# Threshold attention and hash routing on one core: the scale moves from k to the negation, and the copies of the turned weights get a bias

## The chip, the cores and the metric

One Trainium2 chip, one core. The metric is the device time of one launch in microseconds (us); lower is better. The times of the kernel before are three runs on one chip, and one further execution was recorded by the profiler.

## What is computed

For each of 8 x 8 heads (576 queries, 576 keys, 64 dims) the attention keeps only scores within tau of the row's maximum:

```python
scores = 0.125 * q @ k.T
thresh = scores.max(-1) - tau                       # tau = 0.02
scores = where(scores >= thresh, scores, -1e9)
attn   = exp(scores - scores.max(-1))
attn   = attn / (attn.sum(-1) + 1e-9)
x      = (attn @ v), rows of all heads side by side  # 4608 x 512
```

Then each of the 4608 rows goes to one of 8 experts by a hash of its token id (id times an odd constant, modulo 8), and each expert is `relu(xe @ w1[e]) @ w2[e]` with 512 -> 1024 -> 512. A negative tau would keep no score at all; then every weight of a row is equal (all are -1e9), and the kernel handles that case too.

## The kernel before

The attention runs over 32 pairs of heads (`NP`), and each pair over five query tiles. The engines' order within a pair is written out by hand in the table `ORDER`; an entry is a letter, a tile number and a half, and after the @ how many pairs the operation lags. In the order in which one half-tile passes through them the letters are:

- S (`score`): TensorE multiplies q by k into PSUM, 128 x 576 scores. There are two such PSUM tiles (`sc`).
- N (`negate`): VectorE writes the negated scores `ns` and takes their minimum (`nmx`) in the same operation. GpSimd adds `drop` (tau) to give the threshold `thr`.
- E (`expo`): ScalarE computes `exp(-ns + nmx)`; the minimum comes in as the bias, a tile of one number per partition.
- M (`mask`): VectorE zeroes what is over the threshold and sums the row.
- T (`turn_w`): TensorE turns the masked weights into the PSUM tile `tr`. There is only one such tile, so each T has to wait until the copy before has emptied it.
- P (`put_wT`): ScalarE copies `tr` to SBUF (`wT_a`, `wT_b`). A pair has nine such copies: four of 512 columns a partition, five of 640.
- A and C (`av_part`, `av_tail`): TensorE multiplies the turned weights by v. o (`put_oT`), O (`turn_o`) and X (`put_xm`) copy the result, turn it back, and multiply by the reciprocal of the row sums (R).

K (`scale_k`, line 224) is the operation by which ScalarE multiplies the next pair's k tile, 128 x 704, by `k_scale`: 0.125, or 0 where tau is negative. It stands between P00 and P01. For the first pair, VectorE scales one head's half of k and ScalarE the other (lines 802 and 804) before any score is computed.

The routing of tokens (`route`, lines 390 to 560) is cut into pieces by `yield`; each pair issues one or two pieces between its own operations. A piece holds small operations of VectorE and GpSimd. The one-hot table (288 numbers a partition, line 433) is made by eight compares on GpSimd in three pieces. After the last pair come the entries of `DRAIN`, then the experts' layers.

The places that matter below are named by the letters: T21 is the turn of tile 2's second half, P21 its copy, and so on.

Of the kernel before, what the change touches and what calls it, by code (L numbers as in the profile page):

```python
# [9 lines left out]
FP32 = mybir.dt.float32  # L10
# [3 lines left out]
AF = mybir.ActivationFunctionType  # L14
ALU = mybir.AluOpType
# [5 lines left out]
def kernel(  # L21
# [12 lines left out]
    nc = tc.nc  # L34

    B, H, D, S = qT.shape
    N, DIN = out.shape
    E, _, F = w1.shape
    P = 128
# [4 lines left out]
    NTC = N // P  # L44
    SCALE = 1.0 / float(D) ** 0.5
    assert D == 64 and S == 4 * P + 64 and SCALE == 0.125 and E == 8
    S2 = S // 2
    NQ = 4
    TAIL = NQ * P
    NC = 5  # L50
# [32 lines left out]
    consts = ctx.enter_context(tc.tile_pool(name="consts", bufs=1))  # L83
# [7 lines left out]
    iota_f = consts.tile([P, NOV], FP32, name="iota_f")  # L91
# [2 lines left out]
    slot_i = consts.tile([P, NTC], I32, name="slot_i")  # L94
    tid32 = consts.tile([P, NTC, 2], I32, name="tid32")
    tau_in = consts.tile([P, 1], FP32, name="tau_in")
    k_scale = consts.tile([P, 1], FP32, name="k_scale")
    drop = consts.tile([P, 1], FP32, name="drop")

    stok = consts.tile([P, E, NB], I32, name="stok")  # L100
# [52 lines left out]
    with tc.tile_pool(name="a_q", bufs=1) as a_q, \  # L153
# [27 lines left out]
        summed = [0, 0]  # L181
        kts, rss, recs, scs, nss, stats, ws = {}, {}, {}, {}, {}, {}, {}
# [37 lines left out]
            for j in range(2):  # L220
                nc.sync.dma_start(out=v_sb[64 * j:64 * j + 64, 4], in_=rows[TAIL:S])

        def scale_k(p):
            nc.scalar.activation(kts[p][:], kts[p][:], AF.Copy, scale=k_scale[:])

        def heads(n):
            return 1 if TILES[n % NS] == 0 else 2

# [16 lines left out]
        def negate(n, j):  # L245

            if j == 0:
                nmx = a_st.tile([P, 2], FP32, name="nmx")
                stats[n] = [nmx, None]
            sc = scs.pop((n, j))  # L250
            ns = a_ns.tile([P, S], FP32, name="ns")
            nss[n, j] = ns
            nc.vector.tensor_scalar(out=ns[:].rearrange("p (i s) -> p i s", i=2),  # L253
                                    in0=sc[:, :, 0:S2], scalar1=-1.0, scalar2=None,
                                    op0=ALU.mult, op1=ALU.min,
                                    accum_out=stats[n][0][:, j:j + 1])
            if j == heads(n) - 1:
                thr = a_st.tile([P, 2], FP32, name="thr")
                stats[n][1] = thr
                nc.gpsimd.tensor_scalar(out=thr[:, 0:j + 1], in0=stats[n][0][:, 0:j + 1],  # L260
                                        scalar1=drop[:], scalar2=None, op0=ALU.add)
# [44 lines left out]
        def put_wT(n, j, tr):  # L306
            t = TILES[n % NS]
            if t == 0:
                dst = wT[1][:, :, 0:64].rearrange("p (r c) q -> p r c q", r=2)
                nc.scalar.copy(dst, tr[:, :, 0:64 * NC].rearrange("p r (c q) -> p r c q", c=NC))  # L310
                return
            c0 = P * (t - 1) if t < 3 else 64 + P * (t - 3)
            i0, n_c = ((0, 4), (4, NC))[j]
            dst = wT[t // 3][:, i0:i0 + n_c, c0:c0 + P].rearrange("p c (r q) -> p c r q", r=2)
            nc.scalar.copy(dst, tr[:, :, 0:64 * n_c].rearrange("p r (c q) -> p c r q", c=n_c))  # L315

        def av_part(p, g, chunks):

# [39 lines left out]
        def add_eps(p):  # L358

            rec = a_st.tile([P, 2 * NS], FP32, name="rec")  # L360
            rs = rss.pop(p)
            for i, cols in ((0, 9), (9, 1)):
                nc.gpsimd.tensor_scalar(out=rec[:, i:i + cols], in0=rs[:, i - i // 9:i - i // 9 + cols],
                                        scalar1=1e-9, scalar2=None, op0=ALU.add)
            recs[p] = rec

        def put_xm(p):
# [22 lines left out]
        def route():  # L390
# [3 lines left out]
            keep = rt_sb.tile([P, E, NTC], FP32, name="keep")  # L394
            ones_e = rt_sb.tile([P, E], FP32, name="ones_e")
            eid = rt_sb.tile([P, NTC], I32, name="eid")
            eidf = rt_sb.tile([P, NTC], FP32, name="eidf")
            onehot = rt_sb.tile([P, E, NTC], FP32, name="onehot")
            incl = rt_sb.tile([P, E, NTC], FP32, name="incl")
            row = rt_sb.tile([P, E], BF16, name="row")  # L400
# [25 lines left out]

            nc.vector.tensor_scalar(out=eid[:], in0=tid32[:, :, 0], scalar1=E - 1, scalar2=None,
                                    op0=ALU.bitwise_and)
            nc.gpsimd.tensor_copy(eidf[:], eid[:])
            for e0 in range(0, E, 3):  # L430
                yield
                for e in range(e0, min(e0 + 3, E)):
                    nc.gpsimd.tensor_scalar(out=onehot[:, e], in0=eidf[:], scalar1=float(e),
                                            scalar2=None, op0=ALU.is_equal)
            for e in (0, E // 2):
                yield
                part = slice(e, e + E // 2)
# [4 lines left out]
                if e == 0:  # L442
# [5 lines left out]

            tr = av[:, 0, 320:512]
            nc.tensor.matmul(tr[:, 0:E], lhsT=u128[:], rhs=row[:], start=True, stop=True)
            nc.tensor.matmul(tr[:, E:2 * E], lhsT=ones128[:], rhs=row[:], start=True,
                             stop=True)
            nc.vector.tensor_copy(cnt[:], tr[:, 0:2 * E])
            yield

# [2 lines left out]
                                    scalar2=None, op0=ALU.mult)  # L460
# [3 lines left out]
                                    in1=key[:, :, None].to_broadcast([P, E, E]), op=ALU.is_lt)  # L464
# [3 lines left out]
                                    in1=iota_f[:, 0:E, None].to_broadcast([P, E, E]),  # L468
                                    op=ALU.is_equal)
            nc.gpsimd.tensor_tensor(out=pairs[:], in0=pairs[:],  # L470
                                    in1=iota_f[:, None, 0:E].to_broadcast([P, E, E]),
                                    op=ALU.mult)
            for e0, d in STEPS:
                nc.gpsimd.tensor_scalar(out=more_e[:], in0=pos[:], scalar1=float(e0),
                                        scalar2=float(-d), op0=ALU.is_ge, op1=ALU.mult)
                nc.gpsimd.tensor_tensor(out=cnt[:, E:2 * E], in0=cnt[:, E:2 * E], in1=more_e[:],
                                        op=ALU.add)
            nc.gpsimd.tensor_scalar(out=pos[:], in0=pos[:], scalar1=float(1 << 19), scalar2=-1.0,
                                    op0=ALU.mult, op1=ALU.add)
# [5 lines left out]
                                    scalar2=float(P - 1), op0=ALU.add, op1=ALU.max)  # L485
            nc.vector.tensor_scalar(out=ot_i[:], in0=ot_i[:], scalar1=7, scalar2=None,
                                    op0=ALU.logical_shift_right)
# [4 lines left out]
                                         op1=ALU.add)  # L492
# [5 lines left out]
                                    op0=ALU.mult)  # L498
# [4 lines left out]
                                    in1=base[:, :, None].to_broadcast([P, E, NTC]), op=ALU.add)  # L503
# [207 lines left out]
        def begin(p, s):  # L711
# [21 lines left out]
            if s in (3, 4) or NS * p + s == G0 + NS:  # L733
# [2 lines left out]
        ORDER = """N00@0 S01@0 E41@1 N01@0 O@2 X@2 T21@1 S10@0 S11@0 P21@1 T30@1  # L736
                   A001@1 E00@0 P30@1 E01@0 T40@1 M41@1 N10@0 S20@0 P40@1 N11@0 M00@0
                   S21@0 N20@0 M01@0 T41@1 E10@0 P41@1 A023@1 T00@0 N21@0 M10@0 S30@0
                   E20@0 N30@0 E11@0 C@1 P00@0 T01@0 M11@0 K@-1 S40@0 S41@0 P01@0
                   T10@0 o0@1 N40@0 E30@0 A1012@1 N41@0 P10@0 T11@0 S00@-1 E40@0 R@1  # L740
                   M30@0 M20@0 E21@0 A13@1 M40@0 P11@0 M21@0 T20@0 o1@1 P20@0""".split()
        DRAIN = """E41@1 T21@1 P21@1 O@2 X@2 J J T30@1 P30@1 M41@1 A001@1
                   A023@1 T40@1 P40@1 F F T41@1 P41@1 J F F C@1
                   A1012@1 A13@1 o0@1 o1@1 R@1 F F O@1 X@1""".split()
# [2 lines left out]
        def run_op(p, op):  # L747


            what, lag = op.split("@")  # L750
            kind, args = what[0], [int(c) for c in what[1:] if c.isdigit()]
            q = p - int(lag)
            if kind == "N" and args[1] == 0 and 0 <= p < NP:
                begin(p, args[0])
            if kind == "X" and 0 < p < NP and not placed:
                next(pieces)
            if not 0 <= q < NP:
                return
            n = NS * q + args[0] if kind in "SNEMTP" else 0
            if kind == "S":  # L760
                score(n, args[1])
            elif kind == "N":
                negate(n, args[1])
            elif kind == "E":
                expo(n, args[1])
            elif kind == "M":
                mask(n, args[1])
                if n % NS == NS - 1 and args[1] == 1:
                    add_eps(q)
            elif kind == "T":  # L770
                trs[n, args[1]] = turn_w(n, args[1])
            elif kind == "P":
                put_wT(n, args[1], trs.pop((n, args[1])))
            elif kind == "A":
                av_part(q, args[0], args[1:])
            elif kind == "C":
                av_tail(q)
            elif kind == "o":
                put_oT(args[0])
            elif kind == "O":  # L780
                turn_o()
            elif kind == "X":
                put_xm(q)
            elif kind == "R":
                nc.vector.reciprocal(recs[q][:], recs[q][:])
            elif kind == "K" and q > 0:
                scale_k(q)

        with tc.manual_schedule():
            make_identity(nc, ident[:])  # L790
# [2 lines left out]
            for _ in range(17):  # L793
# [3 lines left out]

            nc.vector.tensor_scalar(out=k_scale[:], in0=tau_in[:], scalar1=0.0, scalar2=SCALE,  # L800
                                    op0=ALU.is_ge, op1=ALU.mult)
            nc.vector.tensor_scalar(out=kts[0][:, 0], in0=kts[0][:, 0], scalar1=k_scale[:],
                                    scalar2=None, op0=ALU.mult)
            nc.scalar.activation(kts[0][:, 1], kts[0][:, 1], AF.Copy, scale=k_scale[:])
            nc.vector.tensor_scalar(out=drop[:], in0=tau_in[:], scalar1=0.0, scalar2=3e38,  # L805
                                    op0=ALU.is_lt, op1=ALU.mult)
            nc.vector.tensor_tensor(out=drop[:], in0=drop[:], in1=tau_in[:], op=ALU.max)
            constants()
            next(pieces)
            for p in range(-1, NP):  # L810
# [630 lines left out]
```

## Time and profile before

| | us |
|---|---|
| median of 3 runs | 911.91 (910.63 to 912.23) |
| profiled execution | 911.19 |
| its span in the trace | 909.6 |
| busy in the span: TensorE / VectorE / ScalarE / GpSimd | 891.1 / 754.1 / 535.1 / 455.0 |

The span is what the trace covers; 1.6 us of the profiled execution lie around it. The attention takes the first half: the last operation of `DRAIN` on TensorE is at 461.5 us. Busy times are sums over the whole span. An operation's busy time runs from its start to its end; two of one engine may overlap by some tens of ns, so the distance of two starts can be shorter than the first one's busy time.

### The profile page before, as it was taken

The page shows a single profiled execution, that of the slowest core. Times are in us where ns is not written, and L with a number is a line of the kernel's source. Part 1 is how long each engine was busy: PE and PEld are TensorE (multiplying, and loading weights), DVE is VectorE, ACT ScalarE, POOL GpSimd, SP SyncE. Part 2 cuts the span into 40 slices and gives each one's busy share as a digit, 9 for nine tenths or more (in the row PEclk, how much of TensorE's full clock was granted, in tenths as well). Part 3 has the DMA queues.
Part 4 walks back from the last instruction along what each step waited for, and adds up shares of the span by engine and source line. Part 5 has one row for each costly group of instructions (what it writes and reads, how often), then busy time and mean ns, then how long its engine had stood idle before and what let it go on. Part 6 is the DMA issues. An engine that isn't in the chain of part 4 may idle for free.

```text
span 909.6 us, 21244 instructions
## 1 busy us (share of the span) xinstructions
PE 891.1 (98%) x7663; PEld 662.6 (73%) x7663; DVE 754.1 (83%) x1697; ACT 535.1 (59%) x879; POOL 455.0 (50%) x672
## 2 busy tenths in 40 slices
PE   7999999999999999999999999999999999999996
PEld 4666665666666666666678989889898988989885
DVE  7999999999999999999855786867777686876831
ACT  5999999999999999999812141423214142141321
POOL 3422333346445423444323496884959679390742
PEclk9999999999999999999999999999999999999999
DMA  7455478975544535642101745373353536421001
GB/s 185 108 148 135 122 208 235 247 213 129 135 113 100 139 78 129 159 123 71 34 26 52 212 137 186 121 219 108 90 181 117 194 119 176 153 74 27 32 23 56
DMA packets 114779, 116.30 MB, mean 128 GB/s; under 512 B 28123, under 2 KB 89315, under 8 KB 114672
## 3 DMA queue, kind: packets, MB, share of 16 engines
q1 hardware_dynamic: 105168, 95.69, 38.7%
q0 software_dynamic: 9072, 18.91, 6.6%
q8 instruction: 62, 1.02, 0.5%
q10 hardware_dynamic: 432, 0.31, 0.1%
q14 instruction: 45, 0.37, 0.1%
HBM read 85.13 MB, written 21.44 MB: 117 GB/s over the span
## 4 chain that ended last, share of the span: by engine, by line
PE 29%; POOL 28%; ACT 19%; issue 17%; DVE 3%; DMA 2%; SPq 1%; POOLq 1%; ACTq 0%; DVEq 0%
POOL out_dram L1264 17%; PE av L323 9%; PE sc L242 8%; ACT w L267 8%; POOL stok_odd L1249 7%; PE tr L289 6%; ACT wT_b L315 6%; POOL xg L120 4%; PE sc L663 3%; ACT wT_a L315 2%; ACT wT_b L310 1%; SPq L1294 1%; DMA q<-in_q_dram 1%; DVE ns L253 1%; ACT oT L346 1%
## 5 line engine op out<-in xcount | busy, mean ns | idle before, releaser
L278 DVE SCALAR_TENSOR_TENSOR w<-ns,thr,w 128x576 f32<-128x576 f32 x288 | 225.8, 808 | 0.0
L267 ACT ACTIVATE w<-ns,nmx 128x576 f32<-128x576 f32 x288 | 217.6, 780 | 3.1 <-DVE ns L253 3.1
L253 DVE TENSOR_SCALAR_CACHE_REDUCE ns<-sc 128x576 f32<-128x576 f32 x288 | 211.1, 752 | 3.4 <-PE sc L242 3.4
L260 POOL TENSOR_SCALAR thr<-nmx,drop 128x2 f32<-128x2 f32 (+1 forms) x160 | 95.4, 596 | 223.1 <-DVE ns L253 192.5
L1264 POOL DMA_INDIRECT out_dram<-o_q,qidx x127 | 148.0, 1166 | 114.0 <-DVE o_q L1255 80.4
L242 PE MATMUL sc<-k_sb,q 64*128 64x288 f32 (+1 forms) x1280 | 187.1, 428 | 2.0 <-DVE drop L805 1.0
L289 PEld LDWEIGHTS tr<-ident,w 64*128 64x128 f32 x2624 | 107.2, 138 | 100.8 <-ACT wT_a L315 43.0
L289 PE MATMUL tr<-ident,w 64*128 64x64 f32 x2624 | 139.9, 231 | 7.2 <-ACT wT_a L315 4.1
L242 PEld LDWEIGHTS sc<-k_sb,q 64*128 64x128 f32 (+1 forms) x1280 | 90.9, 178 | 21.6 <-DVE ns L253 10.7
L315 ACT COPY wT_b<-tr 128x512 f32<-128x512 f32 (+1 forms) x128 | 81.8, 639 | 10.6 <-PE tr L289 5.9
L315 ACT COPY wT_a<-tr 128x512 f32<-128x512 f32 (+1 forms) x128 | 81.2, 634 | 3.5 <-PE tr L289 1.4
L323 PE MATMUL av<-wT_b,v 128*64 128x320 f32 x512 | 82.8, 445 | 0.0
L1249 POOL COPY stok_odd<-stok 128x152 int32<-128x152 int32 x157 | 69.6, 444 | 0.6
L323 PE MATMUL av<-wT_a,v 128*64 128x256 f32 x512 | 69.2, 392 | 0.0
L954 PE MATMUL bank<-h,w_sb 128*128 128x288 f32 (+4 forms) x248 | 62.0, 402 | 0.0
L954 PEld LDWEIGHTS bank<-h,w_sb 128*128 128x128 f32 x248 | 58.7, 291 | 0.5
L954 PE MATMUL sc<-h_s,w_s 128*128 128x288 f32 (+2 forms) x224 | 56.6, 406 | 0.0
L323 PEld LDWEIGHTS av<-wT_b,v 128*64 128x64 f32 x512 | 31.1, 136 | 30.4 <-issue 11.9
L978 ACT ACTIVATE h<-h 128x576 f32<-128x576 f32 (+1 forms) x42 | 29.0, 692 | 41.3 <-DVE h L881 41.2
L120 POOL DMA_INDIRECT xg<-x_scratch,gidx_x x35 | 45.2, 1291 | 12.3 <-DVE xq L1286 5.3
L954 PEld LDWEIGHTS sc<-h_s,w_s 128*128 128x128 f32 x224 | 42.7, 195 | 8.7
L987 ACT COPY p<-sc 128x576 f32<-128x576 f32 (+2 forms) x14 | 9.0, 640 | 55.2 <-PE sc L954 55.2
(241 smaller groups left out, 1462.1 us busy)
## 6 DMA issues: line engine op xcount, KB each, us to landing
w_sb<-in_moe_w_dram SPq DMA_DIRECT2D x16, 2048.0 KB
q<-in_q_dram SPq DMA_DIRECT2D x62, 288.0 KB
v<-in_v_dram SPq DMA_DIRECT2D x32, 256.0 KB
x_scratch<-xm SPq DMA_DIRECT2D x32, 256.0 KB
xT<-xq SPq DMA_DIRECT2D x84, 80.0 KB
k_sb<-in_k_dram SPq DMA_DIRECT2D x31, 176.0 KB
k_sb<-in_k_dram SPq DMA_DIRECT2D x32, 144.0 KB
x_scratch<-xg SPq DMA_DIRECT2D x9, 256.0 KB
```

What stands on the lines that cost most here:

```text
L120: return nc.gpsimd.indirect_dma_start(out=dst, out_offset=None, in_=src, in_offset=bass.IndirectOffsetOnAxis(ap=idx, axis=0), bounds_check ...
L242: nc.tensor.matmul(sc[out_rows, i, 0:S2], lhsT=q_sb[rows, h, q0:q1], rhs=k_sb[rows, h, k0:k0 + S2], start=True, stop=True)
L253: nc.vector.tensor_scalar(out=ns[:].rearrange("p (i s) -> p i s", i=2), in0=sc[:, :, 0:S2], scalar1=-1.0, scalar2=None, op0=ALU.mult, op1= ...
L260: nc.gpsimd.tensor_scalar(out=thr[:, 0:j + 1], in0=stats[n][0][:, 0:j + 1], scalar1=drop[:], scalar2=None, op0=ALU.add)
L267: nc.scalar.activation(w, nss[n, j][:], AF.Exp, bias=stats[n][0][:, j:j + 1], scale=-1.0)
L278: nc.vector.scalar_tensor_tensor(out=w, in0=nss.pop((n, j))[:], scalar=stats[n][1][:, j:j + 1], in1=w, op0=ALU.is_le, op1=ALU.mult, accum_ ...
L289: nc.tensor.transpose(dst[:, r, 64 * c:64 * c + 64], src[rows, c0:c0 + P], ident[rows, rows])
L315: nc.scalar.copy(dst, tr[:, :, 0:64 * n_c].rearrange("p r (c q) -> p c r q", c=n_c))
L323: nc.tensor.matmul(av[64 * j:64 * j + 64, g, 0:width], lhsT=v_sb[:, c, 64 * j:64 * j + 64], rhs=wT[g][:, c + 5 * j, 0:width], start=not su ...
L954: nc.tensor.matmul(ps[:, i], lhsT=lhsT, rhs=y[:, c], start=start and c == 0, stop=c == len(lhsTs) - 1, skip_group_check=not start)
L1249: nc.gpsimd.tensor_copy(stok_odd[:], stok[:])
L1264: inst = nc.gpsimd.indirect_dma_start(out=rows[:, :], out_offset=bass.IndirectOffsetOnAxis(ap=idx, axis=0), in_=o_sb, in_offset=None, boun ...
```

## The change

k is no longer scaled. The factor 0.125 goes into the negation's constant (-1.0 becomes -0.125), so K and the two scalings at the start go away, and the scores' matmuls depend directly on the k transfers. A negative tau is now handled behind the mask: `none_kept` is 1 where tau is negative, else 0, and it is added as a bias tile in the nine P copies, which turn from `copy` (the COPY operation) to `activation` with the Identity function. `drop` gets another form for a negative tau, and the added 1e-9 of the row sums becomes a tile `eps`. The one-hot table becomes one VectorE operation, so the routing has two pieces fewer; one piece more comes from a `yield` between two small matmuls and the copy of their result.

```diff
-        def scale_k(p):
-            nc.scalar.activation(kts[p][:], kts[p][:], AF.Copy, scale=k_scale[:])
...
-                                    in0=sc[:, :, 0:S2], scalar1=-1.0, scalar2=None,
+                                    in0=sc[:, :, 0:S2], scalar1=-SCALE, scalar2=None,
                                     op0=ALU.mult, op1=ALU.min,
...
-                nc.scalar.copy(dst, tr[:, :, 0:64 * NC].rearrange("p r (c q) -> p r c q", c=NC))
+                src = tr[:, :, 0:64 * NC].rearrange("p r (c q) -> p r c q", c=NC)
+                nc.scalar.activation(dst, src, AF.Identity, bias=none_kept[:])
...
-            nc.scalar.copy(dst, tr[:, :, 0:64 * n_c].rearrange("p r (c q) -> p c r q", c=n_c))
+            src = tr[:, :, 0:64 * n_c].rearrange("p r (c q) -> p c r q", c=n_c)
+            nc.scalar.activation(dst, src, AF.Identity, bias=none_kept[:])
...
-                                        scalar1=1e-9, scalar2=None, op0=ALU.add)
+                                        scalar1=eps[:], scalar2=None, op0=ALU.add)
...
-            nc.gpsimd.tensor_copy(eidf[:], eid[:])
-            for e0 in range(0, E, 3):
-                yield
-                for e in range(e0, min(e0 + 3, E)):
-                    nc.gpsimd.tensor_scalar(out=onehot[:, e], in0=eidf[:], scalar1=float(e),
-                                            scalar2=None, op0=ALU.is_equal)
+            yield
+            nc.vector.tensor_tensor(out=onehot[:],
+                                    in0=eid[:, None, :].to_broadcast([P, E, NTC]),
+                                    in1=iota_f[:, 0:E, None].to_broadcast([P, E, NTC]),
+                                    op=ALU.is_equal)
...
+            assert summed[0] in (0, NC)
             tr = av[:, 0, 320:512]
...
+            yield
             nc.vector.tensor_copy(cnt[:], tr[:, 0:2 * E])
...
-                   E20@0 N30@0 E11@0 C@1 P00@0 T01@0 M11@0 K@-1 S40@0 S41@0 P01@0
...
+                   E20@0 N30@0 E11@0 C@1 P00@0 T01@0 M11@0 S40@0 S41@0 P01@0 T10@0
...
-            nc.vector.tensor_scalar(out=k_scale[:], in0=tau_in[:], scalar1=0.0, scalar2=SCALE,
+            nc.vector.tensor_scalar(out=drop[:], in0=tau_in[:], scalar1=0.0, scalar2=-3e38,
+                                    op0=ALU.is_lt, op1=ALU.mult)
+            nc.vector.tensor_tensor(out=drop[:], in0=drop[:], in1=tau_in[:], op=ALU.add)
+            nc.vector.tensor_scalar(out=none_kept[:], in0=tau_in[:], scalar1=0.0, scalar2=-1.0,
                                     op0=ALU.is_ge, op1=ALU.mult)
-            nc.vector.tensor_scalar(out=kts[0][:, 0], in0=kts[0][:, 0], scalar1=k_scale[:],
-                                    scalar2=None, op0=ALU.mult)
-            nc.scalar.activation(kts[0][:, 1], kts[0][:, 1], AF.Copy, scale=k_scale[:])
...
+            nc.vector.tensor_scalar(out=none_kept[:], in0=none_kept[:], scalar1=1.0,
+                                    scalar2=None, op0=ALU.add)
+            nc.vector.tensor_scalar(out=eps[:], in0=none_kept[:], scalar1=float(S), scalar2=1e-9,
+                                    op0=ALU.mult, op1=ALU.add)
```

What this moves on the engines. ScalarE, in a pair in the middle of the attention, from P41 to E30. Before:

```order
L315 COPY wT_b<-tr 128x5x128
L267 ACTIVATE w_132<-ns,nmx 128x576
L267 ACTIVATE w_131<-ns,nmx 128x576
L315 COPY wT_a<-tr 128x4x128
L224 ACTIVATE k_sb<-k_sb,k_scale 128x704
L315 COPY wT_a<-tr 128x5x128
L346 COPY oT<-av 128x256
L267 ACTIVATE w_133<-ns,nmx 128x576
```

And the same place in the changed kernel, where line numbers are up to two lower:

```order
L315 ACTIVATE wT_b<-tr,none_kept 128x5x128
L265 ACTIVATE w_133<-ns,nmx 128x576
L265 ACTIVATE w_132<-ns,nmx 128x576
L315 ACTIVATE wT_a<-tr,none_kept 128x4x128
L315 ACTIVATE wT_a<-tr,none_kept 128x5x128
L346 COPY oT<-av 128x256
L265 ACTIVATE w_134<-ns,nmx 128x576
```

K is gone from between P00 and P01, the copies have an operand more, and nothing else changes its place. The next place is VectorE at the start of the program, from the last memset to the first negations. Before:

```order
L609 MEMSET xg_87 128x512
L800 TENSOR_SCALAR k_scale<-tau_in 128x1
L802 TENSOR_SCALAR k_sb<-k_sb,k_scale 128x352
L805 TENSOR_SCALAR drop<-tau_in 128x1
L807 TENSOR_TENSOR drop<-drop,tau_in 128x1
L253 TENSOR_SCALAR ns,nmx<-sc 128x576 x4
```

And in the changed kernel:

```order
L609 MEMSET xg_88 128x512
L798 TENSOR_SCALAR drop<-tau_in 128x1
L800 TENSOR_TENSOR drop<-drop,tau_in 128x1
L801 TENSOR_SCALAR none_kept<-tau_in 128x1
L803 TENSOR_SCALAR none_kept<-none_kept 128x1
L805 TENSOR_SCALAR eps<-none_kept 128x1
L251 TENSOR_SCALAR ns,nmx<-sc 128x576 x4
```

The scaling of k has gone, and five operations of one number per partition stand where four operations stood. The last place is VectorE in the third pair of the changed kernel, where the one-hot table is now made:

```order
L251 TENSOR_SCALAR ns,nmx<-sc 128x576 x2
L429 TENSOR_TENSOR onehot<-eid,iota_f 128x288
L372 TENSOR_TENSOR xm<-av,rec 128x640
L276 SCALAR_TENSOR_TENSOR w_132,rs<-ns,thr,w_132 128x576
L251 TENSOR_SCALAR ns,nmx<-sc 128x576 x2
```

In the kernel before, L372 follows the negations at that place directly, and the table was made by L433 on GpSimd.

## Rows read from the trace of the kernel before

**Rows 1.** Busy time in one steady pair: window, length, PE, PEld, DVE, ACT, POOL; clock, DMA.

```profile
298.17:311.86 13.69, 13.63 (x176) 8.59 (x174) 13.69 (x39) 12.97 (x23) 7.03 (x11) 1.00 0.40 104
```

**Rows 2.** Waits of VectorE up to 470 us: total, times, longest.

```profile
DVE ns L253 <- PE sc L242: 3.4, 11, 0.8
```

**Rows 3.** The chain of waits through the same pair: start, us, what.

```profile
298.17 0.58 ACT wT_b L315
...
299.44 0.68 ACT wT_b L315
...
300.80 0.68 ACT wT_b L310
...
303.53 0.69 ACT wT_b L315
...
305.46 0.58 ACT wT_a L315
...
306.09 0.53 PE tr L289 x10
```

**Rows 4.** TensorE in that pair, in order of time: T21, T30, T40, T10.

```profile
298.81 0.53 PE L289 MATMUL tr<-ident,w 64*128 64x64 f32 x10
...
300.19 0.50 PE L289 MATMUL tr<-ident,w 64*128 64x64 f32 x10
...
301.64 0.46 PE L289 MATMUL tr<-ident,w 64*128 64x64 f32 x8
...
307.48 0.44 PE L289 MATMUL tr<-ident,w 64*128 64x64 f32 x8
```

**Rows 5.** ScalarE around K: P00, K and P01 of the last pair but one.

```profile
429.56 0.57 ACT L315 COPY wT_a<-tr 128x512 f32<-128x512 f32 x1
430.02 0.89 ACT L224 ACTIVATE k_sb<-k_sb,k_scale 128x704 f32<-128x704 f32 x1
430.81 0.69 ACT L315 COPY wT_a<-tr 128x640 f32<-128x640 f32 x1
```

**Rows 6.** ScalarE's groups over the span, shapes apart: busy us, mean ns, idle before.

```profile
L267 ACT ACTIVATE w<-ns,nmx 128x576 f32<-128x576 f32 x288 | 217.6, 780 | 3.1 <-DVE ns L253 3.1
...
L315 ACT COPY wT_a<-tr 128x640 f32<-128x640 f32 x64 | 44.1, 690 | 3.5 <-PE tr L289 1.4
...
L978 ACT ACTIVATE h<-h 128x576 f32<-128x576 f32 x24 | 16.3, 684 | 23.5 <-DVE h L881 23.5
...
L987 ACT COPY p<-sc 128x576 f32<-128x576 f32 x8 | 5.1, 638 | 29.8 <-PE sc L954 29.8
...
L1011 ACT ACTIVATE h<-bank 128x576 f32<-128x576 f32 x4 | 2.6, 653 | 1.9 <-PE bank L954 1.9
```

**Rows 7.** ScalarE in the last pair, which has no K: P00 and P01.

```profile
443.25 0.58 ACT L315 COPY wT_a<-tr 128x512 f32<-128x512 f32 x1
444.50 0.69 ACT L315 COPY wT_a<-tr 128x640 f32<-128x640 f32 x1 [0.68 <-PE tr L289]
```

**Rows 8.** ScalarE in order of time: P20 of the first, fifteenth and last pair.

```profile
18.68 0.58 ACT L315 COPY wT_b<-tr 128x512 f32<-128x512 f32 x1 [0.70 <-PE tr L289]
...
215.73 0.59 ACT L315 COPY wT_b<-tr 128x512 f32<-128x512 f32 x1
...
449.33 0.58 ACT L315 COPY wT_b<-tr 128x512 f32<-128x512 f32 x1 [0.18 <-PE tr L289]
```

**Rows 9.** The start in order of time: k's scaling, first scores, first negation.

```profile
5.11 0.15 DVE L800 TENSOR_SCALAR k_scale<-tau_in 128x1 f32<-128x1 f32 x1 [3.41 <-DMA tau_in<-in_tau_dram]
...
5.72 0.40 DVE L802 TENSOR_SCALAR k_sb<-k_sb,k_scale 128x352 f32<-128x352 f32 x1 [0.46 <-DMA k_sb<-in_k_dram]
...
6.18 1.31 PE L242 MATMUL sc<-k_sb,q 64*128 64x288 f32 x8 [1.03 <-DVE drop L805]
...
7.04 0.76 DVE L253 TENSOR_SCALAR_CACHE_REDUCE ns<-sc 128x576 f32<-128x576 f32 x1 [0.66 <-PE sc L242]
```

**Rows 10.** VectorE's groups up to 480 us: the compare of route that is nearest in size.

```profile
L549 DVE TENSOR_TENSOR keep<-iota_f,oend 128x256 f32<-128x256 f32 x1 | 0.4, 427 | 0.0
```

More of the change, by code (lines that the diff above doesn't have):

```diff
@@ L96 @@
     tau_in = consts.tile([P, 1], FP32, name="tau_in")
-    k_scale = consts.tile([P, 1], FP32, name="k_scale")
+    none_kept = consts.tile([P, 1], FP32, name="none_kept")
+    eps = consts.tile([P, 1], FP32, name="eps")
     drop = consts.tile([P, 1], FP32, name="drop")
@@ L396, in route @@
             eid = rt_sb.tile([P, NTC], I32, name="eid")
-            eidf = rt_sb.tile([P, NTC], FP32, name="eidf")
             onehot = rt_sb.tile([P, E, NTC], FP32, name="onehot")
@@ L738 @@
                    S21@0 N20@0 M01@0 T41@1 E10@0 P41@1 A023@1 T00@0 N21@0 M10@0 S30@0
-                   E20@0 N30@0 E11@0 C@1 P00@0 T01@0 M11@0 K@-1 S40@0 S41@0 P01@0
-                   T10@0 o0@1 N40@0 E30@0 A1012@1 N41@0 P10@0 T11@0 S00@-1 E40@0 R@1
-                   M30@0 M20@0 E21@0 A13@1 M40@0 P11@0 M21@0 T20@0 o1@1 P20@0""".split()
+                   E20@0 N30@0 E11@0 C@1 P00@0 T01@0 M11@0 S40@0 S41@0 P01@0 T10@0
+                   o0@1 N40@0 E30@0 A1012@1 N41@0 P10@0 T11@0 S00@-1 E40@0 R@1 M30@0
+                   M20@0 E21@0 A13@1 M40@0 P11@0 M21@0 T20@0 o1@1 P20@0""".split()
         DRAIN = """E41@1 T21@1 P21@1 O@2 X@2 J J T30@1 P30@1 M41@1 A001@1
@@ L785, in run_op @@
                 nc.vector.reciprocal(recs[q][:], recs[q][:])
-            elif kind == "K" and q > 0:
-                scale_k(q)
         with tc.manual_schedule():
@@ L796 @@
                                 in_=bass.AP(tensor=tau.tensor, offset=0, ap=[[0, P], [1, 1]]))
-            nc.vector.tensor_scalar(out=k_scale[:], in0=tau_in[:], scalar1=0.0, scalar2=SCALE,
+            nc.vector.tensor_scalar(out=drop[:], in0=tau_in[:], scalar1=0.0, scalar2=-3e38,
+                                    op0=ALU.is_lt, op1=ALU.mult)
+            nc.vector.tensor_tensor(out=drop[:], in0=drop[:], in1=tau_in[:], op=ALU.add)
+            nc.vector.tensor_scalar(out=none_kept[:], in0=tau_in[:], scalar1=0.0, scalar2=-1.0,
                                     op0=ALU.is_ge, op1=ALU.mult)
-            nc.vector.tensor_scalar(out=kts[0][:, 0], in0=kts[0][:, 0], scalar1=k_scale[:],
-                                    scalar2=None, op0=ALU.mult)
-            nc.scalar.activation(kts[0][:, 1], kts[0][:, 1], AF.Copy, scale=k_scale[:])
-            nc.vector.tensor_scalar(out=drop[:], in0=tau_in[:], scalar1=0.0, scalar2=3e38,
-                                    op0=ALU.is_lt, op1=ALU.mult)
-            nc.vector.tensor_tensor(out=drop[:], in0=drop[:], in1=tau_in[:], op=ALU.max)
+            nc.vector.tensor_scalar(out=none_kept[:], in0=none_kept[:], scalar1=1.0,
+                                    scalar2=None, op0=ALU.add)
+            nc.vector.tensor_scalar(out=eps[:], in0=none_kept[:], scalar1=float(S), scalar2=1e-9,
+                                    op0=ALU.mult, op1=ALU.add)
             constants()
```

## Prediction

> **What bounds the kernel now.** I first read the busy times of one steady pair [rows 1]: of 13.69 us VectorE is busy 13.69, TensorE 13.63 and ScalarE 12.97. Three engines look full, so shares alone decide nothing. Second, the waits: VectorE, the fullest, waited for scores only 3.4 us in all of the attention [rows 2]. Less work on VectorE could give that back and no more, unless its own operations get fewer. Third, the chain of waits through that pair [rows 3], and here the reader is to see that it runs through ScalarE and TensorE: P20, E41, P21, E00, P30 and so on, to P00, T01, and from there through TensorE's scores and products to the next P20. Six of the nine P copies stand in it: P20, P21, P30, P40, P41, P00. The reason is the single `tr` tile: a turn can't start before the copy of the turn before has ended, and TensorE, which runs in order, holds the next scores behind that turn. So the loop of copies and turns and VectorE's own work take the same 13.69 us, and whatever makes the loop longer shows up in full, while what makes it shorter meets VectorE.
>
> How tight each tie is, by end of the copy and start of the turn behind it [rows 3, 4]. P00 ends at 306.04 and T01 starts at 306.09, so 0.05 us is what the hand-over takes. P20 ends at 298.75, T21 starts at 298.81: slack 0.01. P21 ends at 300.12, T30 starts at 300.19: 0.02. P30 ends at 301.48, T40 starts at 301.64: 0.11. P01 starts 1.25 after P00 [rows 5], so here at 306.71; it lasts 0.69 and ends at 307.40, and T10 starts at 307.48: 0.03. From P41's start at 303.53 to P00's at 305.46 are 1.93 us, which is P41 and two exps back to back (0.69 + 2 x 0.78 [rows 6], less three overlaps of 0.11): no slack either.
>
> **K goes.** 31 operations of 0.89 us leave ScalarE. I take their worth as nothing, and the last pair says so, since it has no K: there too P01 starts 1.25 us after P00 (443.25 to 444.50) and waits for TensorE's turn [rows 7]; with K it starts 1.25 after P00 as well (429.56 to 430.81) [rows 5]. K lies in a hole that T01 makes. If the hole were smaller than it looks, the gain would end at VectorE: the waits of 3.4 us.
>
> **The copies get a bias tile.** This is the term that decides. No row shows an Identity with a bias tile from PSUM, so I bound it. ScalarE's exp with a bias tile takes 780 ns, its relu without one 684, both over 576 numbers from SBUF to SBUF: 96 ns for the bias tile. Relu from PSUM takes 653, a COPY of the same size from PSUM 638: 15 ns for the other operation [rows 6]. Together 0.11 us a copy, 690 becoming about 800. The lower bound is 0.015, if the bias is read while the copy waits for its turn anyway; the upper is 780 - 638 = 0.14, exp against COPY. I take 0.11, since the two differences are of the same operand and the same memory as here.
>
> The Trainium skill bears on this, in "ScalarE: Activation LUTs", section "What ACT_TABLE_LOAD costs": it says that each operand given as one number per partition adds about 93 ns to an ACTIVATE, against constants in the instruction. The trace's 96 ns agree. By that figure the copy would grow by 0.093 + 0.015, and the sum below would come out 0.3 us lower.
>
> On ScalarE's total: nine copies grow by 0.11 each, 1.0 us a pair, and K gives back 0.8, its distance to P01; 12.97 + 0.2 still lies under 13.69. So ScalarE does not become full; what grows is the loop. P20, P21, P41, P00 and P01 pass on 0.11 each less their slack of 0.06 together: 0.49. P30's slack takes its 0.11, and P40 I treat alike. P10 and P11 have products of 1 us and more between them and the next turn. So **0.49 us a pair**. This stands in front of T01, so the scores of tile 4 come late, and VectorE, which has no work of its own to spare there, waits in N40 by that much.
>
> From the first P20 to the last are 31 intervals, 430.65 us [rows 8]; 31 x 13.69 are 424.4. Of the 6.3 more, the first fourteen intervals hold 5.4 (197.05 - 191.66), the later seventeen 0.9. The early part is the routing's small operations on VectorE (and the start). When VectorE waits half a us a pair, they fall into that wait. I take 3.0 us of it as hidden from now on; bounds 0 and 5.4. That gives 31 x 0.49 - 3.0 = +12.2.
>
> **The drain.** Four copies stand between the last P20 and the end of the turns, partly with other work between: +0.4 (4 x 0.11), bounds 0 and 0.6.
>
> **The start.** The first scores waited for VectorE to scale k, from 5.72, when k was there, to 6.18 [rows 9]. Without that they can start at 5.72: -0.45. The five operations on tau take some 0.15 each from 5.11 on, and end by 5.9, before the first negation (7.04 - 0.46 = 6.58). Bounds: 0, if the q transfers landed only then, and -0.9, if only those two of the three k transfers that the first scores read are early.
>
> **The rest.** The one-hot operation on VectorE: 427 ns for 256 numbers [rows 10] makes 0.48 for 288, at the place of a negation's end in the third pair. It falls into VectorE's new wait, so 0; if that cover is gone, +0.4 (less the overlap). GpSimd loses eight compares and nobody waited for them. The 1e-9 as a tile on GpSimd is followed by the reciprocal far later: 0. The routing ends a piece earlier, which moves transfers that nobody waits for. The negation's constant costs nothing.
>
> **Sum.** +12.2 + 0.4 - 0.45 = +12.15 on the profiled execution's 911.19 (span 909.6 and 1.6 around it): 923.3. That execution lies 0.7 under the median of the runs, within their range; on the median, 911.9, the sum makes **924.0**, which I predict.
>
> **Rivals.**
> 1. The bias tile costs only the lower bound, 0.015. The slack of 0.06 takes nearly all of 5 x 0.015; the one-hot then shows with +0.4, the start gives -0.45: 912.4 (911.9 + 0.5 + 0.4 - 0.45), no change. For it: the copies wait for turns, and an operand could be fetched meanwhile. Against it: the exps wait for minima too, and show the full 780.
> 2. Half of the ties give way, since times jitter between pairs and VectorE still sets the pace of some: 31 x 0.25 less 2 us of hidden routing, +0.2 - 0.45: +5.5, 917.4. For it: VectorE is as full as the loop [rows 1], so the ties may be its making. Against it: the chain of waits never passes through VectorE there.
> 3. Faster: K's 0.8 us a pair frees the loop at P01, with the bias tile nearly free. Then VectorE's waits of 3.4 us go and 0.45 at the start: 908.1. It decides only if P01 starts less than 1.25 us after P00; the last pair without K speaks against it.
> 4. The bias tile costs 0.14: 5 x 0.14 - 0.06 + 2 x 0.03 (what P30 and P40 then pass on) = 0.70 a pair, 21.7 - 3.4 + 0.6 - 0.45 = +18.5: 930.4.
>
> **How the numbers follow.** Forecast 0.68; rival 2 0.15; rival 4 0.06; rival 1 0.07; rival 3 0.04. The forecast's own range, with 0.45 to 0.55 a pair and 1 to 4.5 us hidden, is 921 to 927. The range reaches to rival 2 on the lower side and stops between forecast and rival 4 on the upper: 915.5 to 928; rivals 1, 3 and 4 stay outside. A change under 0.2% (1.8 us) can't be told from none here. Faster: rival 3 and a part of rival 1, 0.05; same: 0.07; slower: 0.88.
>
> **What would show it.** The P copies at about 0.80 us (640) and 0.69 (512); a steady pair of about 14.2 us where it was 13.69; VectorE idle by about 0.5 us a pair before N40, put down to the scores; P01 no earlier after P00 than T01 lets it; the first negation near 6.6 us; the experts' half unchanged in length. If the copies stay at 0.70, the forecast is wrong at its main term; if they grow and the pair stays under 14.0, the ties were looser than I read them. A lower clock on TensorE, from its longer waits, would make it slower than all of this.

## The result, and the profile after

| | before | changed |
|---|---|---|
| median, us (four runs each) | 911.46 (910.63 to 912.23) | 924.86 (923.71 to 925.72) |
| profiled execution, span | 911.19, 909.6 | 925.15, 923.6 |
| ratio | | 1.0141, 95% interval 1.0126 to 1.0156 |

The change makes the kernel 1.4% slower, as predicted (924.0, range 915.5 to 928). Its profile is read here in the order of the prediction's views.

The busy time of a steady pair of the changed kernel, in the columns of [rows 1]:

```profile
305.90:320.17 14.27, 14.02 (x176) 8.53 (x174) 13.82 (x39) 13.11 (x22) 7.19 (x11) 1.00 0.42 104
```

The pair has grown from 13.69 to 14.27 us, on the same clock. VectorE, which had no idle time in [rows 1], now has 0.45, and ScalarE is still not full: 13.11 of 14.27. An engine total would not have shown this slowdown coming. ScalarE's operations over the whole span, in the columns of [rows 6]:

```profile
L265 ACT ACTIVATE w<-ns,nmx 128x576 f32<-128x576 f32 x288 | 215.0, 770 | 4.5 <-DVE ns L251 4.5
L315 ACT ACTIVATE wT_b<-tr,none_kept 128x640 f32<-128x640 f32 x64 | 50.8, 794 | 3.0 <-PE tr L287 1.3 <-ACT w L265 0.3
...
L315 ACT ACTIVATE wT_b<-tr,none_kept 128x512 f32<-128x512 f32 x64 | 44.0, 688 | 1.7 <-PE tr L287 1.6
```

A P copy of 640 numbers a partition takes 794 ns where it took 690: +104, predicted +110. The chain of waits through the same pair shows where that lands:

```profile
305.90 0.69 ACT wT_b L315
...
307.27 0.79 ACT wT_b L315
...
308.75 0.79 ACT wT_b L309
...
311.53 0.79 ACT wT_b L315
312.32 1.33 ACT w L265 x2
313.65 0.59 ACT wT_a L315
...
314.28 0.53 PE tr L287 x10
...
320.17 0.69 ACT wT_b L315
```

It is the chain of [rows 3] again: P20, P21, P30, P40, P41, two exps, P00, T01, and by TensorE to the next P20. What is longer in it, by 0.1 us each, are the copies. TensorE's turns in that pair, T21, T30, T40, T01 and T10:

```profile
306.65 0.53 PE L287 MATMUL tr<-ident,w 64*128 64x64 f32 x10
...
308.12 0.52 PE L287 MATMUL tr<-ident,w 64*128 64x64 f32 x10
...
309.59 0.46 PE L287 MATMUL tr<-ident,w 64*128 64x64 f32 x8
...
314.28 0.53 PE L287 MATMUL tr<-ident,w 64*128 64x64 f32 x10 [0.25 <-ACT wT_a L315]
...
315.75 0.46 PE L287 MATMUL tr<-ident,w 64*128 64x64 f32 x8
```

Counted from the start of P20 and set against [rows 3, 4], the delay builds up one tie after another. T21 starts 0.75 after it (before 0.64), T30 2.22 (2.02), T40 3.69 (3.47), T01 8.38 (7.92), T10 9.85 (9.31), and the next P20 14.27 (13.69). So P20 adds 0.11, P21 0.09, P30 0.02, the stretch with P40, P41 and P00 0.24, P01 0.08, and what follows 0.04. Within that stretch P41 starts 5.63 after P20 (before 5.36) and P00 7.65 (7.29; its row 313.55 stands below), so P40 and the exp between it and P41 bring 0.05, P41 0.09 and P00 0.10. On ScalarE, the place where K stood:

```profile
313.55 0.67 ACT L315 ACTIVATE wT_a<-tr,none_kept 128x512 f32<-128x512 f32 x1
314.90 0.79 ACT L315 ACTIVATE wT_a<-tr,none_kept 128x640 f32<-128x640 f32 x1 [0.68 <-PE tr L287]
```

K's hole of [rows 5] is now 0.68 us of idle time, ended by T01. P01 follows P00 by 1.35 us, later than the 1.25 with K, because P00 itself is longer. VectorE's waits up to 470 us, and the one in this pair, before N40:

```profile
DVE ns L251 <- PE sc L240: 10.5, 31, 0.8
```
```profile
315.39 0.76 DVE L251 TENSOR_SCALAR_CACHE_REDUCE ns<-sc 128x576 f32<-128x576 f32 x1 [0.34 <-PE sc L240]
```

VectorE waited for scores 11 times in [rows 2] and 31 times now, once a pair: 10.5 us where it was 3.4. The wait before N40 is 0.34 of the 0.45 us that VectorE is idle in this pair; most of the rest is a gap of 0.11 before N01. Last, P20 of the first, second, fifteenth and last pair, and the start with the one-hot operation:

```profile
18.54 0.69 ACT L315 ACTIVATE wT_b<-tr,none_kept 128x512 f32<-128x512 f32 x1 [0.56 <-PE tr L287]
...
33.87 0.69 ACT L315 ACTIVATE wT_b<-tr,none_kept 128x512 f32<-128x512 f32 x1
...
220.03 0.69 ACT L315 ACTIVATE wT_b<-tr,none_kept 128x512 f32<-128x512 f32 x1
...
463.07 0.69 ACT L315 ACTIVATE wT_b<-tr,none_kept 128x512 f32<-128x512 f32 x1 [0.29 <-PE tr L287]
```
```profile
5.70 1.48 PE L240 MATMUL sc<-k_sb,q 64*128 64x288 f32 x8 [0.45 <-DMA q<-in_q_dram]
...
6.74 0.76 DVE L251 TENSOR_SCALAR_CACHE_REDUCE ns<-sc 128x576 f32<-128x576 f32 x1 [0.76 <-PE sc L240]
```
```profile
L429 DVE TENSOR_TENSOR onehot<-eid,iota_f x1: 452/452/452, 35.0 to 35.0; 128x288 f32<-128x288 int32 x1
```

From the first P20 to the last are 444.53 us, 13.9 more than the 430.65 of [rows 8]; that is the whole slowdown but for some tenths.

### The profile page after: what moved, and what is told of

The parts are those of the page before. It is cut to its first block, busy times and chain, and to the rows that moved or that the text cites. A ratio compares the mean times of both kernels' runs of the same rounds, so it can differ in the third digit from the quotient of the medians.

```text
span 923.6 us, 21173 instructions
## 1 busy us (share of the span) xinstructions
PE 900.8 (98%) x7663; PEld 661.5 (72%) x7663; DVE 757.8 (82%) x1699; ACT 538.9 (58%) x847; POOL 459.3 (50%) x663
## 4 chain that ended last, share of the span: by engine, by line
POOL 27%; PE 27%; ACT 26%; issue 15%; DVE 2%; SPq 1%; DMA 1%; POOLq 1%; ACTq 0%; DVEq 0%
POOL out_dram L1263 16%; ACT w L265 12%; PE av L323 9%; ACT wT_b L315 9%; POOL stok_odd L1248 7%; PE sc L240 7%; PE tr L287 6%; POOL xg L121 4%; PE sc L663 2%; ACT wT_a L315 2%; ACT wT_b L309 2%; SPq L1293 1%; ACT oT L346 1%; DVE ns L251 0%; POOLq L1263 0%
## 5 line engine op out<-in xcount | busy, mean ns | idle before, releaser
L251 DVE TENSOR_SCALAR_CACHE_REDUCE ns<-sc 128x576 f32<-128x576 f32 x288 | 212.0, 753 | 13.6 <-PE sc L240 10.5
L265 ACT ACTIVATE w<-ns,nmx 128x576 f32<-128x576 f32 x288 | 215.0, 770 | 4.5 <-DVE ns L251 4.5
L258 POOL TENSOR_SCALAR thr<-nmx,drop 128x2 f32<-128x2 f32 (+1 forms) x160 | 99.1, 619 | 236.0 <-DVE ns L251 193.5
L287 PEld LDWEIGHTS tr<-ident,w 64*128 64x128 f32 x2624 | 104.8, 138 | 119.7 <-ACT wT_a L315 52.5
L240 PE MATMUL sc<-k_sb,q 64*128 64x288 f32 (+1 forms) x1280 | 184.8, 425 | 1.3 <-DVE ns L251 0.8
L287 PE MATMUL tr<-ident,w 64*128 64x64 f32 x2624 | 142.9, 233 | 12.1 <-ACT wT_a L315 10.5
L315 ACT ACTIVATE wT_a<-tr,none_kept 128x512 f32<-128x512 f32 (+1 forms) x128 | 94.3, 737 | 22.2 <-PE tr L287 21.9
L240 PEld LDWEIGHTS sc<-k_sb,q 64*128 64x128 f32 (+1 forms) x1280 | 93.0, 178 | 16.4 <-DVE ns L251 4.4
L315 ACT ACTIVATE wT_b<-tr,none_kept 128x512 f32<-128x512 f32 (+1 forms) x128 | 94.8, 741 | 4.6 <-PE tr L287 2.9
```

Of the source, the lines that this page charges most:

```text
L240: nc.tensor.matmul(sc[out_rows, i, 0:S2], lhsT=q_sb[rows, h, q0:q1], rhs=k_sb[rows, h, k0:k0 + S2], start=True, stop=True)
L265: nc.scalar.activation(w, nss[n, j][:], AF.Exp, bias=stats[n][0][:, j:j + 1], scale=-1.0)
L287: nc.tensor.transpose(dst[:, r, 64 * c:64 * c + 64], src[rows, c0:c0 + P], ident[rows, rows])
L315: nc.scalar.activation(dst, src, AF.Identity, bias=none_kept[:])
```

## Experiments

Pair lengths below are the distances of two steady P20 or P00 starts. Every ratio is against the kernel before in the same series of runs.

**1. The copies without the bias.** The changed kernel with the copies as before. Here and in runs 2, 5 and 7 only one of the two places at which a copy is issued is shown; the other changes alike.

```diff
-            nc.scalar.activation(dst, src, AF.Identity, bias=none_kept[:])
+            nc.scalar.copy(dst, src)
```

> The changed kernel with the nine P copies as COPY again, without the bias; everything else of the change stays (it leaves out only the handling of a negative tau). Theory (the bias lengthens the loop of copies and turns): the copies fall back to 0.69 and 0.58 us, a steady pair from 14.27 to 13.69 to 13.72 us, the start keeps its 0.3 us, the one-hot on VectorE shows with up to 0.4: 911.6 us, within 1 us of the kernel before. Rival (another part of the change made it slow: the scores waiting directly on the k transfers, the other constant in the negation, or the routing's moved pieces): a pair stays at 14.2 and the time above 920 us.

Measured: 910.3 us (909.12 to 911.34, 12 runs) against 911.77; ratio 0.9986, 0.9977 to 0.9994. The pair is 13.70 us. ScalarE's P00, P01 and the next P00:

```profile
429.18 0.57 ACT L315 COPY wT_a<-tr 128x512 f32<-128x512 f32 x1
430.43 0.69 ACT L315 COPY wT_a<-tr 128x640 f32<-128x640 f32 x1 [0.68 <-PE tr L287]
...
442.88 0.57 ACT L315 COPY wT_a<-tr 128x512 f32<-128x512 f32 x1
```

Everything else of the change together, K's 0.89 us a pair included, is worth 1.5 us in all by the medians (0.5 to 2.1 by the interval), a little more than the 1 us that was expected at most, and nothing in a steady pair. P01 starts 1.25 after P00, as with K. The whole slowdown is in the nine copies.

**2. The operation without the operand.** Identity with a constant in place of the tile.

```diff
-            nc.scalar.activation(dst, src, AF.Identity, bias=none_kept[:])
+            nc.scalar.activation(dst, src, AF.Identity)
```

> The changed kernel with the copies as Identity, but with the bias as a constant of the instruction (0) and not as a tile (it leaves out the handling of a negative tau). Theory (the operand costs 0.096 of the 0.105 us, the operation 0.01 to 0.015): copies of 0.70 and 0.60 us, whose 5 x 0.015 the slack of 0.06 nearly takes; a pair of 13.69 to 13.75 us and 911.6 to 913 us. Rival (the other operation is what costs, whatever its bias): copies of 0.79, a pair of 14.27 and 924.9 us.

Measured: 910.8 us, ratio 0.9998 (0.9989 to 1.0007), pair 13.77. Its copies:

```profile
L315 ACT ACTIVATE wT_b<-tr 128x640 f32<-128x640 f32 x64 | 45.0, 703 | 6.4 <-PE tr L287 3.9 <-ACT w L265 0.3
...
L315 ACT ACTIVATE wT_b<-tr 128x512 f32<-128x512 f32 x64 | 38.3, 598 | 2.9 <-PE tr L287 1.6
```

With a constant a copy of 640 takes 703 ns, with COPY in run 1 693, with the tile 794. So the tile costs 91 ns and the other operation 10. The prediction's two differences, 96 and 15, were both a little large. The pair came out just above the expected 13.69 to 13.75 us and the time below the expected 911.6 to 913. "ScalarE: Activation LUTs" of the Trainium skill, section "What ACT_TABLE_LOAD costs", states about 93 ns for such an operand; the trace agrees, with 91 here from PSUM.

**3 and 4. Which of the nine.** The bias on P30, P40, P10 and P11 alone, or on P20, P21, P41, P00 and P01 alone, the others as `copy`. Run 3's form, of which run 4 has the other list, `((2, 0), (2, 1), (4, 1), (0, 0), (0, 1))`:

```diff
+        def put_copy(n, j, dst, src):
+            if (n % NS, j) in ((3, 0), (4, 0), (1, 0), (1, 1)):
+                nc.scalar.activation(dst, src, AF.Identity, bias=none_kept[:])
+            else:
+                nc.scalar.copy(dst, src)
```

> The changed kernel with the bias on only the four copies whose slack before the next turn is read as 0.1 us or more (P30, P40, P10, P11), the other five as COPY. Theory (only the tied copies count): 0 to 0.04 us a pair, 911.6 to 913 us. Rival (every copy's 0.1 us costs alike, through ScalarE's total): 4/9 of the 13.4 us lost, 917.5 us.

> The changed kernel with the bias on only the five copies read as tied (P20, P21, P41, P00, P01), the other four as COPY. Theory: nearly all of the loss stays: a pair of 14.22 to 14.27 us, 923 to 925 us. Rival (every copy's 0.1 us costs alike): 5/9 of 13.4, 919 us.

Measured: the four slack copies 911.0 us (ratio 0.9992, 0.9983 to 1.0001; pair 13.75), the five tied ones 923.29 us (ratio 1.0130, 1.0115 to 1.0144; pair 14.22). ScalarE with the five, from P20 to the next P20:

```profile
305.19 0.69 ACT L306 ACTIVATE wT_b<-tr,none_kept 128x512 f32<-128x512 f32 x1
...
308.02 0.69 ACT L308 COPY wT_b<-tr 128x640 f32<-128x640 f32 x1
...
312.79 0.67 ACT L306 ACTIVATE wT_a<-tr,none_kept 128x512 f32<-128x512 f32 x1
...
314.15 0.79 ACT L306 ACTIVATE wT_a<-tr,none_kept 128x640 f32<-128x640 f32 x1 [0.68 <-PE tr L287]
...
319.41 0.69 ACT L306 ACTIVATE wT_b<-tr,none_kept 128x512 f32<-128x512 f32 x1
```

Against run 1's 13.70 the five tied copies add 0.52 a pair and the four slack ones 0.05; together 0.57, as the full change does. The slack copies' 0.05 lies just above the expected 0 to 0.04. The same operand at the same price costs 13.0 us in one set of places and 0.7 in the other (923.29 and 911.0 less 910.3). The reading of ties by the end of a copy and the start of the turn behind it is what the two runs test, and it holds. The rival of both expectations, that every copy's 0.1 us costs alike (917.5 and 919 us), falls.

**5. The bias alone, with K left in.** The kernel before, with a tile of zeros as the bias of the nine copies.

```diff
-            nc.scalar.copy(dst, tr[:, :, 0:64 * n_c].rearrange("p r (c q) -> p c r q", c=n_c))
+            src = tr[:, :, 0:64 * n_c].rearrange("p r (c q) -> p c r q", c=n_c)
+            nc.scalar.activation(dst, src, AF.Identity, bias=zero_b[:])
```

> The kernel before with one edit: the nine P copies as Identity with a bias tile of zeros; K stays. Theory (K lies in the hole that T01 makes, also when P00 is longer: P01 starts 1.35 us after P00 in the changed kernel, and P00's 0.58 and K's 0.79 to the next start make 1.37): a pair of 14.27 to 14.30, P01 1.35 to 1.37 after P00, 924 to 926.5 us. Rival (leaving K out paid for a part of the bias, 0.2 us a pair or more): a pair of 14.47 or more and 931 us or more.

Measured: 926.17 us (925.7 to 927.21), ratio 1.0159 (1.0142 to 1.0176), pair 14.28. P00, K and P01, and the P20 on either side:

```profile
307.49 0.69 ACT L318 ACTIVATE wT_b<-tr,zero_b 128x512 f32<-128x512 f32 x1
...
315.15 0.67 ACT L318 ACTIVATE wT_a<-tr,zero_b 128x512 f32<-128x512 f32 x1
315.71 0.88 ACT L225 ACTIVATE k_sb<-k_sb,k_scale 128x704 f32<-128x704 f32 x1
316.50 0.79 ACT L318 ACTIVATE wT_a<-tr,zero_b 128x640 f32<-128x640 f32 x1
...
321.77 0.69 ACT L318 ACTIVATE wT_b<-tr,zero_b 128x512 f32<-128x512 f32 x1
```

With K between them, P01 starts 1.35 after P00, exactly as in the changed kernel, which has no K. In run 1 VectorE's own work fills the pair, which could have hidden a gain from K; here the loop is longer than that work, and the pair is still that of the changed kernel. So K is worth nothing in a steady pair on either side.

**6. The factor elsewhere.** The kernel before without K: the factor, -0.125 or 0, goes as a tile into VectorE's negation, where a negative tau is then handled too. The copies stay.

```diff
-                                    in0=sc[:, :, 0:S2], scalar1=-1.0, scalar2=None,
+                                    in0=sc[:, :, 0:S2], scalar1=k_scale[:], scalar2=None,
...
-                   E20@0 N30@0 E11@0 C@1 P00@0 T01@0 M11@0 K@-1 S40@0 S41@0 P01@0
+                   E20@0 N30@0 E11@0 C@1 P00@0 T01@0 M11@0 S40@0 S41@0 P01@0
...
```

> The kernel before without K and without the scalings at the start: the factor (-0.125, or 0 for a negative tau) is read by the negation as a tile of one number per partition; copies, routing and everything else as before, all of the reference computed. Theory (such an operand is free on VectorE, where the mask has one already; K is worth nothing; the start gives 0.3): negation of 0.75 us, a pair of 13.69, 910 to 911.5 us. Rival (the operand costs on VectorE as on ScalarE, 0.096 us): negation of 0.85, VectorE's own work 13.6 + 0.86 = 14.5 a pair, some 935 us.

Measured: 922.31 us (922.0 to 923.11), ratio 1.0121 (1.0104 to 1.0137). Both expectations missed. The negation's group on VectorE in the kernel before, then here with its accumulator's reading, and the busy time of a pair:

```profile
L253 DVE TENSOR_SCALAR_CACHE_REDUCE ns<-sc 128x576 f32<-128x576 f32 x288 | 211.1, 752 | 3.4 <-PE sc L242 3.4
```
```profile
L253 DVE TENSOR_SCALAR_CACHE_REDUCE ns<-sc,k_scale 128x576 f32<-128x576 f32 x288 | 225.5, 805 | 1.6 <-PE sc L242 1.4
...
L253 DVE DVE_READ_ACCUMULATOR ns<-sc,k_scale 128x1 f32 x288 | 21.8, 76 | 0.0
```
```profile
299.40:313.50 14.10, 14.05 (x178) 8.53 (x174) 14.10 (x39) 12.29 (x21) 7.11 (x12) 1.00 0.45 113
```

A tile costs VectorE something as well: 805 ns where the constant took 752, +53, neither nothing nor ScalarE's 96. Nine of them, with the accumulator's reading 6 ns shorter (82 to 76), make 9 x 0.047 = 0.42 a pair; the pair grew by 0.41, from 13.69 to 14.10, and VectorE is busy for all of it. The fault in the expectation was to treat the operand as free on the engine that had no slack. With waits of 3.4 us in all [rows 1, 2], VectorE has next to nothing to give, and what it gets shows in full.

**7. The operand twice.** The changed kernel with a tile of ones as the copies' scale as well.

```diff
-            nc.scalar.activation(dst, src, AF.Identity, bias=none_kept[:])
+            nc.scalar.activation(dst, src, AF.Identity, bias=none_kept[:], scale=one_s[:])
```

> The changed kernel with a second operand tile in the nine P copies: a scale of ones beside the bias. Theory (each operand tile lengthens a copy by 0.093, and the loop by that times the tied copies): copies of 0.89 and 0.78 us; five tied copies, and P30 and P40, whose slack is used up, make seven: a pair of 14.73 (five) to 14.92 us (seven), 939 to 945 us. Rival (a second operand is read along with the first): copies of 0.79, a pair of 14.27, 924.9 us.

Measured: 950.67 us (949.98 to 951.76) against 917.21 for the kernel before in that series, which was on a chip where that kernel too took longer; ratio 1.0362 (1.0334 to 1.0389). The expected 939 to 945 us are missed as they stand; 1.0362 of the 911.46 us of the kernel before would be 944.5. The copies, the P20 at either end of an early pair, and a later stretch:

```profile
L316 ACT ACTIVATE wT_b<-tr,none_kept,one_s 128x640 f32<-128x640 f32 x64 | 56.6, 884 | 6.3 <-PE tr L288 5.0 <-issue 0.3
```
```profile
168.45 0.78 ACT L316 ACTIVATE wT_b<-tr,none_kept,one_s 128x512 f32<-128x512 f32 x1
...
183.34 0.78 ACT L316 ACTIVATE wT_b<-tr,none_kept,one_s 128x512 f32<-128x512 f32 x1
```
```profile
255.21:270.82 15.61, 14.37 (x176) 8.54 (x178) 13.91 (x39) 13.82 (x21) 7.64 (x11) 1.00 0.42 103
```

The second tile costs 90 ns, like the first. From 34 to 213 us eleven of the twelve pairs take 14.9 us, like the one shown with 14.89. That is 0.62 more, as if nearly seven copies passed their growth on (0.62 / 0.09). That fits what was expected: once the first operand has used up the slack, the copies that had some are tied too. No run puts the second operand on some of the copies alone, so which seven isn't shown. Not expected was what follows. From 228 to 368 us the pairs take 15.1 to 15.8 us with the same operations on TensorE and VectorE and at the granted clock of 1.00, and of the eight behind them only two are back at 14.9. In the long pairs the chain of waits runs through TensorE's turns and products rather than through the exps behind P20 and P21. What sets it off isn't settled. On this chip the kernel before took 5.5 us longer too, and no trace of it there was kept, so the long pairs may belong to the chip as well as to the edit.

**8. K on another engine.** The kernel before, with K on GpSimd.

```diff
-            nc.scalar.activation(kts[p][:], kts[p][:], AF.Copy, scale=k_scale[:])
+            nc.gpsimd.tensor_scalar(out=kts[p][:], in0=kts[p][:], scalar1=k_scale[:],
+                                    scalar2=None, op0=ALU.mult)
```

> The kernel before with K on GpSimd in place of ScalarE, at the same place of the order; everything of the reference is computed. Theory (K cost nothing on ScalarE): a pair of 13.69 us and 911 to 912 us, provided that GpSimd's multiplication of 704 numbers (some 2 us, from 0.79 us for 288 in the routing) doesn't hold up the thresholds behind it; if it does, VectorE waits for thr by up to 1 us a pair and the time goes up to 940. Rival (ScalarE's 0.8 us a pair was worth something): a pair under 13.6 and less than 909 us.

Measured: 932.76 us (932.18 to 936.34) against 917.21; ratio 1.0163 (1.0140 to 1.0186). It is the expectation's second case, in which K holds up the thresholds. K on GpSimd, its queue in one pair, and what VectorE now waits for up to 480 us:

```profile
L224 POOL TENSOR_SCALAR k_sb<-k_sb,k_scale 128x704 f32<-128x704 f32 x31 | 63.8, 2057 | 0.0
```
```profile
308.49 2.06 POOL L224 TENSOR_SCALAR k_sb<-k_sb,k_scale 128x704 f32<-128x704 f32 x1
310.72 1.03 POOL L568 DMA_INDIRECT slot_scratch<-tok,slot_i  x1 [0.17 <-issue]
311.80 0.31 POOL L261 TENSOR_SCALAR thr<-nmx,drop 128x2 f32<-128x2 f32 x1
```
```profile
DVE w L279 <- POOL thr L261: 12.9, 22, 1.3
DVE ns L254 <- PE sc L243: 9.6, 21, 2.0
```

K takes 2.06 us there, and a threshold that M needs stands in GpSimd's queue behind it: 22 waits of VectorE, 12.9 us. Five more waits before M, 3.9 us, are put down to no releaser. But it isn't K alone. In 15 of the 31 pairs an operation of the routing that issues a transfer, 1.0 to 1.6 us long, stands between K and the threshold, as in the pair shown; 14.4 of these 16.8 us of waiting fall there. Where the threshold follows K directly, M waits 0.19 us at most. GpSimd is busy for only 55% of the span (515.3 of 934.7 us) and still can't take K at this place, since what counts is what else is queued there. Where K costs nothing is the hole on ScalarE in which it stood. No version here handles a negative tau and is faster than the kernel before; run 1, which is 0.14% faster, leaves that out.

## Why the prediction was right

- **The bias tile's price** was predicted at 0.11 a copy; it is 0.104 (794 less 690), 0.091 of it the tile and about 0.01 the other operation (run 2). The lower bound, a tile read while the copy waits anyway (rival 1), falls: the copies in the chain show the full price.
- **0.49 us a pair** was too small; it is 0.575 (two pairs of 14.27 and 14.26, less 13.69). The five ties were sized right: in the pair above they bring 0.11, 0.09, 0.09, 0.10 and 0.08, 0.47 in all against 0.49. Their slack was smaller than the 0.06 that I took off, since after P20, P21 and P01 (ends 306.59, 308.06, 315.69) the turns still start 0.06 later (306.65, 308.12, 315.75), but the copies grew by a little less than 0.11 too. What was mis-sized is what I put at nothing. P30 brings 0.02 and P40 with the exp behind it 0.05. I treated P40 like P30, whose slack is before the next turn, but P41 follows P40 on ScalarE with one exp between them. Run 3, with the tile on P30, P40, P10 and P11 alone, has 0.05 a pair. The last 0.04 arise between T10 and the next P20, and their cause isn't settled: it takes 4.42 us from T10 to there, before 4.38, and also 4.42 in run 4, where P10 and P11 have no bias. Run 4's 0.52 is about the five ties and this. VectorE's wait stands before N40, where it was put, but with 0.34 us and not 0.49.
- **Routing hidden, 3.0 us**, with bounds of 0 and 5.4. Of the 444.53 us, 31 pairs of 14.265 are 442.2, which leaves 2.3 where [rows 8] left 6.3: 4.0 are gone, 3.6 of them in the first fourteen intervals. How much of it the wait hides isn't settled. In runs 1, 2 and 3, with the changed routing and hardly any wait, the same sum leaves 4.1, 4.1 and 4.7 (428.81 less 31 x 13.70; 430.98 less 31 x 13.77; 430.94 less 31 x 13.75), so about half may lie in the other pieces of routing (run 1's first P20 came 1.6 us later than here). In run 5, with the routing of before and the wait, it leaves 2.1 (444.76 less 31 x 14.28), but its first P20 came 1.8 us later than here, which may hold a part.
- These two errors run against each other: 31 x 0.575 - 4.0 = 13.8 between the first and the last P20, predicted 12.2. That the median fell within 0.9 us of 924.0 is in part luck: the slowdown is 13.4 us where the sum had 12.15, and the kernel before came out at 911.46 where the prediction started from 911.9.
- **The drain**: from the last P20 to the experts' first VectorE operation 12.56 us, before 12.24. +0.32, predicted +0.4.
- **The start**: the first scores start at 5.70, as predicted (5.72), but the first negation gained 0.30, not 0.45 ([rows 9]: 7.04, now 6.74). The eight matmuls took 1.48 us where they took 1.31. That differs between executions: in run 1, which starts with the same operations, they took 2.15 us and the first negation came at 7.31, later than in the kernel before. So a gain of 0.30 is shown for this execution only. At the first P20, 18.54 against 18.68, 0.14 of it is left. Then -0.14, +13.88 between the P20s and the drain's +0.32 make +14.06, against 13.96 between the two profiled executions.
- **K worth nothing**: shown by runs 1 and 5 together. Rival 3 falls with it.
- **The one-hot operation** takes 452 ns (predicted 480) at 35.0 us. The pair in which it lies, from P20 at 33.87 to the next at 48.17, takes 14.30, 0.03 over a steady one: hidden, as predicted.
- **Rival 2**, half of the ties giving way at 917.4, and rival 4, 0.14 a copy, fall with runs 3 and 4 and with the copies' own 0.104. What rival 2 had for it, that VectorE is as full as the loop, is true, and run 6 shows it: but two limits of equal length didn't share the delay here, and the longer one set the pace.

## What to carry to other kernels

Where one small buffer is passed to and fro between two engines, the operations that fill and empty it are a chain. In this kernel a tenth of a microsecond on each was paid nearly in full by the pair, whatever the engine's total said, and K's 0.89 us, which lay in a hole of that chain, was free, so that its removal was worth nothing. So before an operand is moved from a rare operation to a frequent one, ask of each instance whether the next engine waits for its end: here the same 0.1 us was worth 13 us in five places and 0.7 in four. When several engines are equally full, moving the work to the one that has no slack only changes which of them is late (run 6).

## What the runs showed of the hardware that was not expected

- A tile of one number per partition in place of a constant costs VectorE's negation 53 ns (752 to 805, 128x576 from PSUM), where it costs ScalarE's copy 91 (703 to 794) and a second one 90 (794 to 884).
- One multiplication of 128x704 numbers by such a tile takes 0.89 us on ScalarE and 2.06 on GpSimd.
- In run 7 pairs of the same operations took from 14.9 to 15.8 us within one execution, at a granted clock of 1.00; the cause is open.
